# Retention and two feed-forward layers on one core: where the weight conversions and the retention stand, whose engine decays, and how wide the activations are

## The chip, the core and the metric

The kernel runs on one core of a Trainium2 chip. Its engines are TensorE (PE, matrix products; PEld is its weight load), VectorE (DVE), ScalarE (ACT), GpSimd (POOL) and SyncE (SP, which here issues all DMAs). They run side by side, each takes its own instructions strictly in a fixed order, and they wait for each other through semaphores. The metric is the device time of one execution in microseconds (us), as the median of several runs: 1741.69 us before (three runs, 1738.77 to 1744.80).

## What is computed

For 8 sequences of 576 tokens with 8 heads of 64 columns, the scores of q and k are scaled, multiplied by a decay that depends on the distance of two tokens, and multiplied with v (no softmax). The result, 4608 tokens of 512 columns, goes through two feed-forward layers of 2048 inner columns. The four weight matrices arrive as 64-bit floats (8.4 MB each).

```python
scores = scale * np.matmul(q, k.transpose(0, 1, 3, 2))
gamma = 1.0 - 2.0 ** (-5.0 - np.arange(H, dtype=np.float32))
Dmat = np.where(rel >= 0, gamma[:, None, None] ** rel[None, :, :], 0.0)
x = np.matmul(scores * Dmat, v)            # then (4608, 512)
h = x @ w1_in;  g = h - np.tanh(h);  x = g @ w1_out
h = x @ w2_in;  g = h * (1.0 / (1.0 + np.exp(-1.702 * h)));  out = g @ w2_out
```

## The kernel before, in words

**Retention.** Each sequence is cut into four chunks of 128 tokens and one of 64, so there are 40 chunks. A chunk is loaded (kT, qT, v, k: `att_load`), q and v are multiplied by powers of gamma on POOL (`att_decay`, lines 362 and 364), PE makes the scores pj (line 374), DVE multiplies them by the causal mask into pm (line 379), PE makes the output op from pm and v (391) and from the state S of the chunks in front (396), and the update up of S (413), which DVE adds (417). A chunk therefore waits for the one before it in its sequence through S. The output goes to DRAM (x_d), the first 512 tokens stay on the chip.

**Conversion of the weights.** DVE and ACT turn the two 32-bit words of each 64-bit weight into a 32-bit float, find each block's largest magnitude and split the block into two 16-bit parts, hi and lo. A unit is one DMA of 512 columns on 128 partitions (512 KB, 32 units a layer): ACT takes the magnitude (172), DVE clamps and shifts (177, 180), joins (187, 189), and later ACT writes hi (262) and DVE lo (263). After a block (four units) the largest value is spread over the partitions by POOL (`partition_all_reduce`, 121), and the small steps of `scale` (127 to 117) make a power of two from it. Layer 2 also forms sums of quarter blocks (221 to 224) for a scheme with seven products in place of eight, and its splits are lines 237 and 238.

**Layers.** Tokens are taken in 9 tiles of 512. In layer 1 a tile has 16 steps: 12 matmuls make h of 128 inner columns (541, three 16-bit products for each of four parts), ACT and DVE compute g = h - tanh(h) and split it (`act1`, lines 556 to 568), and 12 matmuls add it to the output (660), at least LAG = 2 steps later. In layer 2 a tile has 8 pair steps: 42 matmuls of 256 columns (587), `act2` (600 to 615), and 24 matmuls (637). Before a tile starts, its x is scanned, scaled and split (`prep_steps`).

**Order.** Before layer 1 stand the first FIRST = 4 chunks and the conversion of w1_in, 8 units in flight; its steps run under `urgent`. The conversion of w1_out and the other 36 chunks follow within layer 1: its first LAG0 = 8 steps carry the whole conversion of w1_out, also urgent, and mm_out starts after them; each step takes one or two of the three parts of a chunk. The conversion of layer 2 is spread over what is left of layer 1 but its last LAST2 = 20 steps, with one block buffer (`wb2`, bufs 1). A scheduler then fixes the order on each engine: by written order as priority, with an instruction moved up where its engine would else stand idle by the scheduler's own costs.

Of the kernel before, what the change touches and what calls it, by code (L numbers as in the profile page):

```python
# [49 lines left out]
FIRST = 4  # L50
LAST2 = 20
NIP = 3
NF1 = 3
NF0 = 8
LAG0 = 8
RATE0 = 2.0
RATE = 1.0
# [21 lines left out]
def retention_two_ffn(ctx: ExitStack, tc: tile.TileContext, q, k, v, w1i, w1o, w2i, w2o,  # L79
                      qt, kt, dq_d, dv_d, mask_d, out):  # L80
# [17 lines left out]
    tp = pool("tp", 2)  # L98
    ep = pool("ep", 4)
# [33 lines left out]
    for l in (1, 2):  # L133
        o = Obj()
        for nm, n in (("s_in", 4), ("inv_in", 4), ("s_out", 4), ("inv_out", 4), ("rs", 1), ("top", 16)):
            setattr(o, nm, cp.tile([P, n], F32, name=f"{nm}{l}"))
        o.wih, o.wil, o.woh, o.wol = {}, {}, {}, {}
        L[l] = o

    def conversion(l, kinds, w_in, w_out, fp, wb, wp):  # L140
# [5 lines left out]
        units = [(kind, b, u) for kind in kinds for b in range(4) for u in range(4)]  # L146
        f64s, blocks, red, sums = {}, {}, {}, {}

        def load(i):
            if i >= len(units):  # L150
                return
            kind, b, u = units[i]
            f = f64s[i] = fp.tile([P, 512, 2], I32, tag="f64", name="f64")
            if kind == "i":
                src = w_in.bitcast(I32)[:, b * 1024 + u * 256 : b * 1024 + u * 256 + 256]
            else:
                src = w_out.bitcast(I32)[u * 512 : u * 512 + 512, b * 256 : b * 256 + 256]
            SP.dma_start(f.rearrange("p (a b) c -> p a (b c)", a=4), src.rearrange("(a p) f -> p a f", p=P))

        def view(kind, w, u):  # L160
            return w[:, :, u * P : u * P + P] if kind == "i" else w[:, u * 4 : u * 4 + 4, :]

        def magnitude(i):
# [19 lines left out]
        def join(i):  # L183
            kind, b, u = units[i]
            wi = view(kind, blocks[kind, b][0], u).bitcast(I32)
            f = f64s.pop(i).rearrange("p (a b) c -> p a b c", a=4)
            V.scalar_tensor_tensor(out=wi, in0=f[:, :, :, 1], scalar=SIGN_TOP, in1=wi,  # L187
                                   op0=ALU.bitwise_and, op1=ALU.bitwise_or)
            V.scalar_tensor_tensor(out=wi, in0=f[:, :, :, 0], scalar=29, in1=wi,
                                   op0=ALU.logical_shift_right, op1=ALU.bitwise_or)  # L190

        def reduce(kind, b):
            mx = blocks[kind, b][1]
            if kind == "i":
                V.tensor_copy(out=o.top[:, 4 * b : 4 * b + 4], in_=mx)
# [51 lines left out]
        def split(kind, b, u):  # L247
            w = blocks[kind, b][0]
            if kind == "i":
# [14 lines left out]
            if u == 3:  # L264
# [13 lines left out]
    def conversion_steps(l, kinds, w_in, w_out, fp, nf, wb, ahead, wp, also=None):  # L278
# [4 lines left out]
        def start():  # L283
            for i in range(nf):
                load(i)
                if i == 1 and also:
                    also()
# [3 lines left out]
        for n, (kind, b) in enumerate(blocks):  # L291
            prev = blocks[n - 1] if n else None
            for u in range(4):
                i = 4 * n + u

                def one(i=i, u=u):
# [3 lines left out]
                    if ahead or u < 3:  # L300
# [16 lines left out]
            if not ahead or n == len(blocks) - 1:  # L317
# [5 lines left out]
                else:  # L323
                    steps += [lambda kind=kind, b=b, u=u: split(kind, b, u) for u in range(4)]
# [4 lines left out]
    x_done = [0]  # L329
    x_first = []  # L330
    early = [True]
# [5 lines left out]
    def att_load(b, n):  # L337
# [5 lines left out]
        for nm, src in (("kT", kt), ("qT", qt)):  # L343
            t = ip.tile([P, NPAIR, P], F32, tag=f"in_{nm}", name=f"{nm}_{b}_{n}", bufs=2 if nm == "kT" else NIP)
            SP.dma_start(t[:, :, :T], src[b, :, :, s0 : s0 + T].rearrange("h p s -> p h s"))
            setattr(a, nm, t)
        for nm, src in (("v", v), ("k", k)):
            if nm == "k" and n + 1 == len(CHUNKS):
                continue
            t = ip.tile([P, H, D], F32, tag=f"in_{nm}", name=f"{nm}_{b}_{n}")  # L350
            rows = src[b, :, s0 : s0 + T, :].rearrange("h p d -> p h d")
            if T == P:
                SP.dma_start(t, rows)
            else:
                for j in range(2):
                    SP.dma_start(t[64 * j : 64 * j + 64, :NPAIR, :], rows[:, j::2, :])
            setattr(a, nm, t)

    def att_decay(b, n):
        s0, T = CHUNKS[n]  # L360
        a = att[b, n]
        G.tensor_tensor(out=a.qT[:, :, :T], in0=a.qT[:, :, :T], in1=dq[:, :, s0 : s0 + T], op=ALU.mult)
        nh = H if T == P else NPAIR
        G.tensor_tensor(out=a.v[:, :nh], in0=a.v[:, :nh], in1=dv[:, n, :nh].to_broadcast([P, nh, D]), op=ALU.mult)

    def att_scores(b, n, pp):
# [9 lines left out]
        for s_ in pj:  # L376
            t = ap.tile([P, NPAIR, P], F32, tag="pm", name="pm", bufs=3)
# [4 lines left out]
    def att_values(b, n, pp):  # L382
# [39 lines left out]
        x_done[0] = g0 + T  # L422
# [122 lines left out]
    def act1(t, c, h):  # L545
# [3 lines left out]
        u = tp.tile([P, TT], F32, tag="u", name="u")  # L549
        w = tp.tile([P, TT], F32, tag="w", name="w")  # L550
        th = tp.tile([P, TT], F32, tag="t", name="t")
        d = tp.tile([P, TT], F32, tag="z", name="d")
        mk = tp.tile([P, TT], U8, tag="m", name="m")
        gh = gp[-1].tile([P, TT], F16, tag="gh", name="gh")
        gl = gp[-1].tile([P, TT], BF16, tag="gl", name="gl")
# [8 lines left out]
        gtile[1, t, c] = gh, gl  # L564
        A.activation(out=gh, in_=w, func=AF.Copy, scale=sg)  # L565

        def finish():
            V.scalar_tensor_tensor(out=gl, in0=w, scalar=sg, in1=gh, op0=ALU.mult, op1=ALU.subtract)  # L568

        return finish  # L570
# [21 lines left out]
    def act2(t, p, prods):  # L592
# [4 lines left out]
        h0 = tp.tile([P, TT], F32, tag="u", name="h0")  # L597
        h1 = tp.tile([P, TT], F32, tag="w", name="h1")
# [9 lines left out]
        for x, h in enumerate((h0, h1)):  # L608

            g = tp.tile([P, TT], F32, tag="tz"[x], name=f"g{x}")  # L610
            gh = gp[-1].tile([P, TT], F16, tag="gh", name="gh")
            gl = gp[-1].tile([P, TT], F16, tag="gl", name="gl")
# [8 lines left out]
    def mm_y(t, p):  # L621
# [9 lines left out]
        for m in range(4):  # L631
# [6 lines left out]
            if last:  # L638
                c = tp.tile([P, 4, P], F32, tag="z", name="c")
# [259 lines left out]
```

## Time and profile before

| | us |
|---|---|
| median of the runs (three) | 1741.69 |
| the profiled execution, its own time | 1743.8 |
| its span, first to last instruction | 1742.0 |
| PE busy in the span | 1632.8 (94%) |
| DVE busy | 1242.1 (71%) |
| ACT busy | 856.1 (49%) |
| POOL busy | 124.8 (7%) |

The profile is of one execution. The span leaves 1.8 us of its own time outside, and that execution is 2.1 us above the median. A row of a timeline gives an instruction's start and duration; two instructions of one engine overlap a little at their ends, so what one takes in a full row is the distance from its start to the next start. Busy time of a group counts each instant once.

### The profile page before, as it was taken

The page shows a single profiled execution, that of the slowest core. Times are in us where ns is not written, and L with a number is a line of the kernel's source. Part 1 is how long each engine was busy: PE and PEld are TensorE (multiplying, and loading weights), DVE is VectorE, ACT ScalarE, POOL GpSimd, SP SyncE. Part 2 cuts the span into 40 slices and gives each one's busy share as a digit, 9 for nine tenths or more (in the row PEclk, how much of TensorE's full clock was granted, in tenths as well). Part 3 has the DMA queues.
Part 4 walks back from the last instruction along what each step waited for, and adds up shares of the span by engine and source line. Part 5 has one row for each costly group of instructions (what it writes and reads, how often), then busy time and mean ns, then how long its engine had stood idle before and what let it go on. Part 6 is the DMA issues. An engine that isn't in the chain of part 4 may idle for free.

```text
span 1742.0 us, 26391 instructions
## 1 busy us (share of the span) xinstructions
PE 1632.8 (94%) x10429; PEld 929.1 (53%) x10512; DVE 1242.1 (71%) x2462; ACT 856.1 (49%) x1383; POOL 124.8 (7%) x120
## 2 busy tenths in 40 slices
PE   1468889999999999999999999999999999999998
PEld 1334444544544454454444456666666666666665
DVE  4779889869898978697797674747566574746453
ACT  1245466556665656566676663434434243434332
POOL 1222100111111111100000000000000000000000
PEclk7679999999999999999999999999999999999999
DMA  9347315344444535322510120101010010100000
GB/s 287 104 119 202 107 61 151 104 120 136 140 143 139 158 88 161 82 71 81 207 49 1 46 86 27 49 1 49 1 49 29 21 50 1 49 1 25 1 25 25
DMA packets 203132, 141.42 MB, mean 81 GB/s; under 512 B 109184, under 2 KB 187136, under 8 KB 200448
## 3 DMA queue, kind: packets, MB, share of 16 engines
q1 hardware_dynamic: 203008, 139.74, 26.7%
q8 instruction: 82, 1.34, 0.3%
q14 instruction: 42, 0.34, 0.1%
HBM read 100.91 MB, written 38.80 MB: 80 GB/s over the span
## 4 chain that ended last, share of the span: by engine, by line
PE 74%; DVE 14%; issue 4%; DMA 4%; ACT 1%; SPq 1%; POOL 1%; POOLq 0%; DVEq 0%
PE yp L637 21%; PE pr L587 19%; PE y L660 15%; PE h L541 14%; DVE w L563 1%; DVE gl L568 1%; DVE w L561 1%; DVE w L562 1%; PE op L391 1%; DVE d L560 1%; PE pj L374 1%; DVE w L187 1%; PE op L396 1%; DVE pm L379 1%; DVE w L177 1%
## 5 line engine op out<-in xcount | busy, mean ns | idle before, releaser
L587 PEld LDWEIGHTS <-ws 128*128 128x128 f16 x3024 | 295.9, 98 | 52.3
L541 PE MATMUL h<-xh,wih 128*128 128x512 f16 x576 | 220.2, 383 | 14.2 <-DVE d L560 8.5
L660 PE MATMUL y<-gh,wol 128*128 128x512 f16 x576 | 218.7, 380 | 4.7 <-issue 0.7
L541 PE MATMUL h<-xh,wil 128*128 128x512 f16 x576 | 220.1, 382 | 0.0
L541 PE MATMUL h<-xl,wih 128*128 128x512 f16 x576 | 220.0, 382 | 0.0
L637 PE MATMUL yp<-woh,gh 128*128 128x512 f16 x576 | 218.3, 379 | 0.0
L637 PE MATMUL yp<-wol,gh 128*128 128x512 f16 x576 | 218.3, 379 | 0.0
L637 PE MATMUL yp<-woh,gl 128*128 128x512 f16 x576 | 217.7, 379 | 0.0
L587 PE MATMUL pr<-th,ws 128*128 128x256 f16 x1152 | 212.5, 273 | 0.0
L660 PE MATMUL y<-gh,woh 128*128 128x512 f16 x576 | 200.8, 383 | 9.3 <-ACT gh L565 5.1
L613 ACT ACTIVATE g<-h,isig 128x512 f32<-128x512 f32 x144 | 102.1, 714 | 206.3 <-DVE h L605 206.2
L565 ACT ACTIVATE gh<-w,sg 128x512 f16<-128x512 f32 x144 | 103.9, 721 | 193.4 <-DVE w L563 176.9
L541 PEld LDWEIGHTS <-wih 128*128 128x128 f16 x1152 | 112.4, 98 | 149.9 <-issue 20.0
L660 PE MATMUL y<-gl,woh 128*128 128x512 bf16 x493 | 187.7, 381 | 1.6 <-DVE gl L568 1.4
L660 PEld LDWEIGHTS <-woh 128*128 128x128 f16 x1152 | 109.1, 98 | 138.1 <-issue 9.0
L637 PEld LDWEIGHTS <-gh 128*128 128x128 f16 x1152 | 112.7, 98 | 119.5
L587 PE MATMUL pr<-bh,ws 128*128 128x256 f16 x864 | 165.5, 273 | 0.0
L615 DVE SCALAR_TENSOR_TENSOR gl<-g,sg,gh 128x512 f16<-128x512 f32 x144 | 107.5, 750 | 75.8 <-ACT gh L614 75.7
L587 PE MATMUL pr<-tl,ws 128*128 128x256 f16 x576 | 157.0, 273 | 0.0
L560 DVE SCALAR_TENSOR_TENSOR d<-h,isig,t 128x512 f32<-128x512 f32 x144 | 107.3, 745 | 64.2 <-ACT t L557 64.1
L568 DVE SCALAR_TENSOR_TENSOR gl<-w,sg,gh 128x512 bf16<-128x512 f32 x144 | 115.6, 803 | 47.4 <-ACT gh L565 47.1
L601 DVE TENSOR_TENSOR h<-h,pr 128x256 f32<-128x256 f32 x72 | 30.2, 419 | 154.5 <-ACT h L600 154.5
(110 smaller groups left out, 2467.4 us busy)
## 6 DMA issues: line engine op xcount, KB each, us to landing
f<-in_moe_w_in SPq DMA_DIRECT2D x32, 512.0 KB, 5.1
f<-in_moe_w_out SPq DMA_DIRECT2D x32, 512.0 KB, 4.6
yd<-ev SPq DMA_DIRECT2D x36, 256.0 KB, 2.8
yf<-yd SPq DMA_DIRECT2D x9, 1024.0 KB, 4.8
out<-c SPq DMA_DIRECT2D x36, 256.0 KB, 2.0
kT<-t_k SPq DMA_DIRECT2D x32, 256.0 KB, 3.0
qT<-t_q SPq DMA_DIRECT2D x32, 256.0 KB, 3.5
v<-in_v SPq DMA_DIRECT2D x32, 256.0 KB, 4.0
```

Source lines behind the costliest of these rows:

```text
L177: V.tensor_scalar(out=w, in0=w, scalar1=HI_MOST, scalar2=HI_LEAST, op0=ALU.min, op1=ALU.max, accum_out=mx[:, u : u + 1])
L187: V.scalar_tensor_tensor(out=wi, in0=f[:, :, :, 1], scalar=SIGN_TOP, in1=wi, op0=ALU.bitwise_and, op1=ALU.bitwise_or)
L541: PE.matmul(h, w, x[:, kd, :], start=n == 0, stop=n == 3 * KD - 1)
L560: V.scalar_tensor_tensor(out=d, in0=h, scalar=isig, in1=th, op0=ALU.mult, op1=ALU.subtract)
L565: A.activation(out=gh, in_=w, func=AF.Copy, scale=sg)
L568: V.scalar_tensor_tensor(out=gl, in0=w, scalar=sg, in1=gh, op0=ALU.mult, op1=ALU.subtract)
L587: PE.matmul(ps, w, x[:, xi, k, :], start=i == 0, stop=i == 5)
L601: V.tensor_tensor(out=h0[:, l_], in0=h1[:, l_], in1=p2, op=ALU.add)
L613: A.activation(out=g, in_=h, func=AF.Gelu_apprx_sigmoid, scale=isig)
L615: V.scalar_tensor_tensor(out=gl, in0=g, scalar=j.sg[:, 0:1], in1=gh, op0=ALU.mult, op1=ALU.subtract)
L637: PE.matmul(y, a[:, cs], b, start=p == 0 and x == 0 and r == 0, stop=last and x == 1 and r == 2)
L660: PE.matmul(ys[m], a, b, start=first and i == 0, stop=last and i == 2)
```

## The change

Twenty chunks in place of four now stand before layer 1, with the conversions of both matrices of layer 1 (`"io"`), and the first tile's preparation; nothing is urgent any more. The other twenty chunks stand in the first twenty pair steps of layer 1, all three parts of a chunk in one step, and only behind them, when their buffers are free, does the conversion of layer 2 begin, now with two block buffers. A conversion unit is twice as wide (1 MB, 1024 columns; 16 units a layer; four in flight), with runs of 2 KB in DRAM for w_in. The host lays q, k and v out so that a chunk's tile has runs of 2 KB (1 KB in the short chunk) for each partition. The decay of q goes from POOL to DVE, that of v from POOL to eight pieces of 64 columns on ACT. Layer 1's activation works on pairs: the three instructions that read h stay at 512 columns, the other six take 1024; so do the last three of layer 2. The output's tiles c share two wide buffers.

```diff
-FIRST = 4
-LAST2 = 20
-NIP = 3
-NF1 = 3
-NF0 = 8
-LAG0 = 8
-RATE0 = 2.0
-RATE = 1.0
+FIRST = 20
+LAST2 = 10
+NIP = 4
+NF0 = 4
...
-        units = [(kind, b, u) for kind in kinds for b in range(4) for u in range(4)]
+        units = [(kind, b, u) for kind in kinds for b in range(4) for u in range(2)]
...
-            f = f64s[i] = fp.tile([P, 512, 2], I32, tag="f64", name="f64")
+            f = f64s[i] = fp.tile([P, 1024, 2], I32, tag="f64", name="f64")
...
+        if not b:
+            SP.dma_start(dq[:, :, s0 : s0 + T], dq_d[:, :, s0 : s0 + T])
+        for nm, src, h in (("kT", kt, NPAIR), ("qT", qt, NPAIR), ("v", v, H if T == P else NPAIR), ("k", k, H)):
...
-        G.tensor_tensor(out=a.qT[:, :, :T], in0=a.qT[:, :, :T], in1=dq[:, :, s0 : s0 + T], op=ALU.mult)
-        nh = H if T == P else NPAIR
-        G.tensor_tensor(out=a.v[:, :nh], in0=a.v[:, :nh], in1=dv[:, n, :nh].to_broadcast([P, nh, D]), op=ALU.mult)
+        V.tensor_tensor(out=a.qT[:, :, :T], in0=a.qT[:, :, :T], in1=dq[:, :, s0 : s0 + T], op=ALU.mult)
+        for h in range(H if T == P else NPAIR):
+            A.activation(out=a.v[:, h], in_=a.v[:, h], func=AF.Copy, scale=dv[:, n, h])
...
-    def act1(t, c, h):
+    def wide(tag, dt=F32, to=None, **kw):
...
+    def act1(t, c, hs):
+
         j = jobs[1, t]
         blk = c // 4
         isig, sg = j.isig[:, blk : blk + 1], j.sg[:, 0:1]
-        u = tp.tile([P, TT], F32, tag="u", name="u")
...
-        A.activation(out=u, in_=h, func=AF.Square, scale=isig)
-        A.activation(out=th, in_=h, func=AF.Tanh, scale=isig)
+        u, w, th, d, mk = wide("u"), wide("w"), wide("t"), wide("z"), wide("m", U8)
+        gh, gl = wide("gh", F16, gp[-1]), wide("gl", BF16, gp[-1])
+        for x, h in enumerate(hs):
+            A.activation(out=u[:, x], in_=h, func=AF.Square, scale=isig)
+            A.activation(out=th[:, x], in_=h, func=AF.Tanh, scale=isig)
+            V.scalar_tensor_tensor(out=d[:, x], in0=h, scalar=isig, in1=th[:, x], op0=ALU.mult, op1=ALU.subtract)
         A.activation(out=w, in_=u, func=AF.Square, scale=SQ, bias=sqb)
         A.activation(out=mk, in_=th, func=AF.Square, scale=MASK_SCALE)
-        V.scalar_tensor_tensor(out=d, in0=h, scalar=isig, in1=th, op0=ALU.mult, op1=ALU.subtract)
         V.scalar_tensor_tensor(out=w, in0=w, scalar=LEVEL, in1=u, op0=ALU.add, op1=ALU.mult)
         V.tensor_tensor(out=w, in0=w, in1=th, op=ALU.mult)
         V.copy_predicated(w, mk, d)
-        gtile[1, t, c] = gh, gl
         A.activation(out=gh, in_=w, func=AF.Copy, scale=sg)
...
+        V.scalar_tensor_tensor(out=gl, in0=w, scalar=sg, in1=gh, op0=ALU.mult, op1=ALU.subtract)
+        for x in range(2):
+            gtile[1, t, c + x] = gh[:, x], gl[:, x]
...
-
-            g = tp.tile([P, TT], F32, tag="tz"[x], name=f"g{x}")
-            A.activation(out=g, in_=h, func=AF.Gelu_apprx_sigmoid, scale=isig)
-            A.activation(out=gh, in_=g, func=AF.Copy, scale=j.sg[:, 0:1])
-            V.scalar_tensor_tensor(out=gl, in0=g, scalar=j.sg[:, 0:1], in1=gh, op0=ALU.mult, op1=ALU.subtract)
-            gtile[2, t, 2 * p + x] = gh, gl
+
+        A.activation(out=g, in_=h, func=AF.Gelu_apprx_sigmoid, scale=isig)
+        A.activation(out=gh, in_=g, func=AF.Copy, scale=j.sg[:, 0:1])
+        V.scalar_tensor_tensor(out=gl, in0=g, scalar=j.sg[:, 0:1], in1=gh, op0=ALU.mult, op1=ALU.subtract)
+        for x in range(2):
+            gtile[2, t, 2 * p + x] = gh[:, x], gl[:, x]
...
-        with ExitStack() as ps0:
-            fp = pool("fp", NF0, to=ps0, side="right")
-            wb = pool("wb", 2, to=ps0, side="right")
-            conv = conversion_steps(1, "i", w1i, w1o, fp, NF0, wb, True, wp1, constants)
-            pp = pool("ps0", 2, PSUM, to=ps0), {"s": "s", "v": "v", "u": "u"}
+        with ExitStack() as scope:
+            def constants():
...
+            fp = pool("fp", NF0, to=scope, side="right")
+            wb = pool("wb", 2, to=scope, side="right")
+            conv = conversion_steps(1, "io", w1i, w1o, fp, NF0, wb, True, wp1, constants)
+            pp = pool("ps0", 2, PSUM, to=scope), {"s": "s", "v": "v", "u": "u"}
             conv.popleft()()
...
+            jobs[1, 0].scale_y = scale_y
+            conv.extend(pre)
+            rate = len(conv) / (FIRST + 2)
...
-            for i in range(-2, len(chunks)):
-                acc += per
+            for i in range(-2, FIRST):
+                acc += rate
                 todo = int(acc)
...
-                if i + 2 < len(chunks):
+                if i + 2 < FIRST:
                     att_decay(*chunks[i + 2])
-                for _ in range(cuts[0]):
-                    urgent(conv.popleft())
-                if 0 <= i + 1 < len(chunks):
+                if 0 <= i + 1 < FIRST:
                     att_scores(*chunks[i + 1], pp)
-                for _ in range(cuts[1]):
-                    urgent(conv.popleft())
+                for _ in range(todo):
+                    conv.popleft()()
                 if i >= 0:
                     att_values(*chunks[i], pp)
...
+                att_load(*beyond[i + NIP])
...
+        tp = pool("tp", 2)
+        ep = pool("ep", 4)
+        gp.append(pool("gp", LAG + 1))
...
-        steps = [(1, t, c) for t in range(NTILE) for c in range(KF)]
-                l, t, c = steps[i]
-                fin = act1(t, c, mm_in(l, t, c, ps_h))
+        steps = [(t, p) for t in range(NTILE) for p in range(KF // 2)]
+                t, p = steps[i]
+                act1(t, 2 * p, [mm_in(1, t, 2 * p + x, ps_h) for x in range(2)])
+                if p == 1:
...
-                todo_a += RATE0 if early[0] else RATE
-                while bg and todo_a >= 1:
-                    wb = pool("wb2", 1, to=att_scope, side="right")
+                if bg:
+                    for _ in range(3):
+                        bg.popleft()()
+                elif conv2 is None:
+                    psa_scope.close()
+                    att_scope.close()
+                    fp = pool("fp2", 2, to=conv_scope, side="right")
+                    wb = pool("wb2", 2, to=conv_scope, side="right")
...
                     conv2 = conversion_steps(2, "io", w2i, w2o, fp, 2, wb, False, stg)
                     rate2 = len(conv2) / (n1 - LAST2 - i)
                 if conv2:
```

On POOL, at the start of the program, decays and all-reduces alternated (in `v_1_186` the first number is the chunk, and ISA without operands is a call that precedes the library's routine or the decay):

```order
L121 ISA
L121 ISA arw<-m_223 128x1
L362 ISA
L362 TENSOR_TENSOR qT_1_184<-qT_1_184,dq 128x512
L121 ISA
L121 ISA arw<-m_324 128x1
L364 ISA
L364 TENSOR_TENSOR v_1_186<-v_1_186,dv 128x512
```

In the changed kernel the same place reads:

```order
L115 ISA
L115 ISA arw<-m_235 128x1
L115 ISA arw<-m_354 128x1
L115 ISA arw<-m_562 128x1
L115 ISA arw<-m_700 128x1
L272 ISA rs_113<-m 128x1
```

The decays have left POOL; what is left there is one kind of instruction.

On PE, the first matmuls of layer 1 (line 541 before, 528 after) stood behind the first sequence and the first chunk of the second (`v_0_454`):

```order
L391 MATMUL op<-pm,v_4_373 64x64 x4
L396 MATMUL op<-qT_4_371,S 64x64 x2
L374 MATMUL pj_885<-qT_0_452,kT_0_450 128x128 x4
L374 MATMUL pj_886<-qT_0_452,kT_0_450 128x128 x4
L391 MATMUL op<-pm,v_0_454 64x128 x8
L413 MATMUL up<-v_0_454,k_0_456 64x64 x8
L541 LDWEIGHTS wih_0_266
L541 MATMUL h<-xh_0_615,wih_0_266 128x512
```

Now they stand behind the whole fourth sequence and the scores of the first chunk of the fifth (`qT_0_1432`):

```order
L379 MATMUL op<-pm,v_4_1364 64x64 x4
L384 MATMUL op<-qT_4_1362,S 64x64 x4
L379 MATMUL op<-pm,v_4_1364 64x64 x4
L384 MATMUL op<-qT_4_1362,S 64x64 x2
L362 MATMUL pj_1697<-qT_0_1432,kT_0_1430 128x128
L362 MATMUL pj_1698<-qT_0_1432,kT_0_1430 128x128
...
L528 LDWEIGHTS wih_0_286
L528 MATMUL h<-xh_0_1572,wih_0_286 128x512
```

Twenty chunks are in front of the first matmul of line 528, where six were in front of that of line 541.

On DVE, in the conversion of layer 2 inside layer 1, instructions of one conversion block stood between those of the activation (d, w, gl; `w_4843` is the block):

```order
L195 COPY top_126<-mx_4844 128x4
L197 TENSOR_REDUCE m_5376<-mx_4844 128x1
L189 SCALAR_TENSOR_TENSOR w_4843<-f_4903,w_4843 128x4x128
L568 SCALAR_TENSOR_TENSOR gl<-w,sg,gh 128x512
L562 TENSOR_TENSOR w<-w,t 128x512
L187 SCALAR_TENSOR_TENSOR w_4843<-f_5055,w_4843 128x4x128
L270 TENSOR_REDUCE tm<-top_126 128x1
L560 SCALAR_TENSOR_TENSOR d<-h,isig,t 128x512
L379 TENSOR_TENSOR pm<-pj_4543,mask_131 128x4x64
L563 COPY_PREDICATED w<-m,d 128x512
L561 SCALAR_TENSOR_TENSOR w<-w,u 128x512
```

In the changed kernel a like stretch (z is the former d, `w_5258` the block):

```order
L550 COPY_PREDICATED w<-m,z 128x1024
L108 TENSOR_SCALAR p_4991<-p_4991 128x1
L108 TENSOR_SCALAR p_5250<-p_5250 128x1
L236 SCALAR_TENSOR_TENSOR wsl<-wsum,s_in_115,wsh 128x1024
L175 TENSOR_SCALAR w_5258,mx_5259<-w_5258 128x4x256
L549 TENSOR_TENSOR w<-w,t 128x1024
L175 TENSOR_SCALAR w_5258,mx_5259<-w_5258 128x4x256
L109 TENSOR_SCALAR s_in_115<-p_4991 128x1
L111 TENSOR_SCALAR inv_in_116<-p_4991 128x1
L109 TENSOR_SCALAR sg<-p_5250 128x1
L111 TENSOR_SCALAR sg<-p_5250 128x1
L552 SCALAR_TENSOR_TENSOR gl<-w,sg,gh 128x1024
```

Before, the 32 units of layer 2 (line 177) are spread over the steps 17 to 94 of the 144 on DVE; now the 16 wide ones (line 175) stand between the pair steps 20 and 39 of the 72.

## Rows read from the trace of the kernel before

**Rows 1.** Busy time by stage, all engines; columns: window, length, engines, granted clock, DMA share, GB/s
```profile
0.00:100.00 100.00, 30.59 (x310) 24.10 (x312) 58.38 (x146) 22.99 (x38) 19.10 (x22) 0.68 0.69 189
160.00:300.00 140.00, 126.98 (x738) 62.64 (x749) 124.39 (x250) 81.58 (x133) 18.58 (x17) 0.98 0.42 120
300.00:860.00 560.00, 550.68 (x3516) 272.14 (x3571) 468.76 (x865) 340.96 (x556) 70.45 (x60) 1.00 0.43 127
860.00:1000.00 140.00, 139.37 (x647) 64.38 (x658) 111.37 (x184) 95.21 (x155) 1.90 (x2) 1.00 0.11 37
```
**Rows 2.** The chain that ended last, two pieces of layer 2: start, us, what
```profile
1072.17 5.18 PE yp L637 x24
1077.35 4.59 PE pr L587 x42
```
**Rows 3.** By stage, weight loads of line 541, then line 660, engine PEld
```profile
300.00:860.00 560.00, 101.81 (x1044) 1.00 0.43 127
...
300.00:860.00 560.00, 97.78 (x1045) 1.00 0.43 127
```
**Rows 4.** By stage, matmuls of line 391, engine PE
```profile
0.00:100.00 100.00, 10.44 (x86) 0.68 0.69 189
...
300.00:860.00 560.00, 33.15 (x416) 1.00 0.43 127
```
**Rows 5.** Waits of PE from 0 to 160 us: total, times, longest
```profile
PE pj L374 <- POOL qT L362: 50.2, 4, 16.5
```
**Rows 6.** Timeline of POOL: start, us, engine, line, operation [idle before, releaser]
```profile
26.77 0.38 POOL L121 PARTITION_ALL_REDUCE arw<-m  x1 [9.32 <-issue]
34.02 2.12 POOL L362 TENSOR_TENSOR qT<-qT,dq 128x512 f32<-128x512 f32 x1 [6.88 <-issue]
...
1119.85 0.35 POOL L121 PARTITION_ALL_REDUCE arx<-m  x1 [77.65 <-DVE m L458]
```
**Rows 7.** Timeline of DVE at 1119.5 us
```profile
1119.54 0.15 DVE L458 TENSOR_REDUCE m<-mxx 128x1 f32<-128x2 f32 x1
```
**Rows 8.** Timeline of DVE, a stretch without a gap
```profile
404.42 0.68 DVE L177 TENSOR_SCALAR_CACHE_REDUCE w<-w 128x512 f32<-128x512 f32 x1
...
405.02 0.68 DVE L561 SCALAR_TENSOR_TENSOR w<-w,u 128x512 f32<-128x512 f32 x1
405.63 0.75 DVE L180 TENSOR_SCALAR w<-w 128x512 int32<-128x512 int32 x2
406.30 0.74 DVE L568 SCALAR_TENSOR_TENSOR gl<-w,sg,gh 128x512 bf16<-128x512 f32 x1
...
407.56 1.28 DVE L187 SCALAR_TENSOR_TENSOR w<-f,w 128x512 int32<-128x512 int32 x2
408.77 0.74 DVE L560 SCALAR_TENSOR_TENSOR d<-h,isig,t 128x512 f32<-128x512 f32 x1
409.43 0.92 DVE L563 COPY_PREDICATED w<-m,d 128x512 f32<-128x512 uint8 x1
```
**Rows 9.** Timeline of DVE, then of POOL, at 390 us
```profile
390.35 0.87 DVE L238 SCALAR_TENSOR_TENSOR wsl<-w,s_in,wsh 128x256 f16<-128x256 f32 x2
391.14 1.28 DVE L238 SCALAR_TENSOR_TENSOR wsl<-wsum,s_in,wsh 128x1024 f16<-128x1024 f32 x1
392.34 3.08 DVE L238 SCALAR_TENSOR_TENSOR wsl<-w,s_in,wsh 128x256 f16<-128x256 f32 x3
...
391.30 2.25 POOL L362 TENSOR_TENSOR qT<-qT,dq 128x512 f32<-128x512 f32 x1 [10.55 <-DMA qT<-t_q]
```
**Rows 10.** Busy time of all engines in 5 us (columns as in rows 1)
```profile
10.00:15.00 5.00, 0.00 (x0) 0.00 (x0) 0.41 (x1) 0.00 (x0) 0.00 (x0) 1.00 1.02 350
```
**Rows 11.** Groups by line, one of ACT: count, busy us, mean ns, idle before
```profile
L419 ACT COPY S<-up 128x256 f32<-128x256 f32 x8 | 3.0, 369 | 0.0
```
**Rows 12.** By stage, matmuls of line 541, engine PE
```profile
100.00:120.00 20.00, 7.66 (x24) 0.70 0.31 80
```
**Rows 13.** Timeline, the last DVE instruction before the end
```profile
1737.77 1.34 DVE L640 TENSOR_TENSOR c<-yp,iy 128x512 f32<-128x512 f32 x2 [1.60 <-DMA out<-c]
```

More of the change, by code (lines that the diff above doesn't have):

```diff
@@ L283, in start @@
         def start():
+            if also:
+                also()
             for i in range(nf):
                 load(i)
-                if i == 1 and also:
-                    also()
             magnitude(0)
@@ L292, in conversion_steps @@
             prev = blocks[n - 1] if n else None
-            for u in range(4):
-                i = 4 * n + u
+            for u in range(2):
+                i = 2 * n + u
                 def one(i=i, u=u):
@@ L323, in conversion_steps @@
                 else:
-                    steps += [lambda kind=kind, b=b, u=u: split(kind, b, u) for u in range(4)]
+                    steps += [lambda kind=kind, b=b, u=u: split(kind, b, u) for u in range(2)]
         return deque(steps)
     att = {}
-    x_done = [0]
     x_first = []
-    early = [True]
     def ps_tile(pp, stage, name):
@@ L638, in mm_y @@
             if last:
-                c = tp.tile([P, 4, P], F32, tag="z", name="c")
+                if m % 2 == 0:
+                    both = wide("z")
+                c = both[:, m % 2].rearrange("p (b d) -> p b d", b=4)
                 V.tensor_tensor(out=c, in0=y.rearrange("p (b d) -> p b d", b=4), in1=iy, op=ALU.mult)
-                SP.dma_start(out[t * TT + m * P : t * TT + m * P + P, :], c.rearrange("p b d -> p (b d)"))
+                SP.dma_start(out[t * TT + m * P : t * TT + m * P + P, :], both[:, m % 2])
         if last:
@@ L690, in tile_slots @@
     def tile_slots(t):
-        sp = xp if t % 2 else wp2[0]
-        return [(sp, tag + (str(x) if t % 2 == 0 else "")) for x in range(2) for tag in ("xh", "xl")]
+        if t % 2:
+            return (xp, "xh"), (xp, "xl"), (xp, "xh"), (xp, "xl")
+        return (wp1, "wih0"), (wp1, "wil0"), (wp1, "wih1"), (wp1, "wil1")
     chunks = [(b, n) for b in range(B) for n in range(len(CHUNKS))]
-    later = chunks[FIRST:]
-    chunks = chunks[:FIRST]
-    beyond = chunks + later + [(B, 0)] * 8
+    beyond = chunks + [(B, 0)] * NIP
     if True:
-        def urgent(f):
-            with tc.high_priority(offset=URGE):
-                f()
+        gp = []
         att_scope = ctx.enter_context(ExitStack())
@@ L768, in retention_two_ffn, with first @@
         bg = deque()
-        for i, ch in enumerate(later):
-            nxt = beyond[len(chunks) + i + 3]
-            def first(ch=ch, nxt=nxt):
-                att_load(*nxt)
+        for i, ch in enumerate(chunks[FIRST:]):
+            def first(ch=ch, nxt=beyond[FIRST + i + NIP - 1] if i else None):
+                if nxt:
+                    att_load(*nxt)
                 att_decay(*ch)
@@ L887 @@
         add(f"in_{name}", a.view(np.int64) if a.dtype == np.float64 else a)
[L888 to L891 removed]
+    for name, turned in (("q", True), ("k", True), ("k", False), ("v", False)):
+        x = np.asarray(inputs[name])
+        rows = []
+        for s0, T in CHUNKS:
+            c = x[:, :, s0 : s0 + T]
+            if turned:
+                c = c.reshape(B, NPAIR, 2, T, D).transpose(0, 2, 4, 1, 3)
+            elif T == P:
+                c = c.transpose(0, 2, 1, 3)
+            else:
+                c = c.reshape(B, NPAIR, 2, T, D).transpose(0, 2, 3, 1, 4)
+            rows.append(c.reshape(B, T * DM))
+        add(f"{'t' if turned else 'n'}_{name}", np.ascontiguousarray(np.concatenate(rows, axis=1)))
     for name, a in const_arrays().items():
```

204 lines of the change are left out of this document (69 added, 135 removed).

## The prediction

> **What bounds the kernel now.** I read four views in this order. First the busy time by stage: from 300 us on PE is busy in 550.7 of 560 us, then in 139.4 of 140, while up to 100 us it is busy in only 30.6 of 100 [rows 1]. So PE's work sets the end, and a change can only move the time in which PE does none of it. Second, what that work takes: 24 matmuls of 512 columns 5.18 us, a pair's 42 of 256 columns 4.59 [rows 2]. Layer 1 is 144 steps of 5.18 us (12 + 12 matmuls), 746 us; layer 2 is 72 pairs of 4.59 + 5.18, 703 us. In 300 to 860 us stand 1044 + 1045 weight loads of the two layer lines [rows 3], 451 us of matmuls, and 416 of the 16 records that line 391 has a chunk [rows 4], 26 chunks: (550.7 - 451) / 26 = 3.84 us a chunk on PE. The floor is 746 + 703 + 40 x 3.84 = 1603 us. The span of 1742 lies 139 above it.
>
> Third, where these 139 us are. Up to 100 us line 391 has 86 records, 5.4 chunks, 21 us of the floor's work: 79 lost. From 300 to 860: 9.3. At the end about 6 (the last evictions wait and store from 1737.8 on [rows 13]). The difference, 45, fell between 100 and 300, where the conversion of w1_out ran beside layer 1's activation and DVE was busy in 124.4 of the last 140 us [rows 1]. Fourth, why: PE waited 50.2 us for POOL's decay of q in four waits [rows 5], and POOL itself did nothing then: each change between its decays and its all-reduce has 6 to 9 us in front of it in which nothing is waited for that the profile shows [rows 6]. With no decay near, the all-reduce starts 0.2 us behind the DVE instruction that feeds it [rows 6, 7]. [...]
>
> **The change, part by part.** Since the PE floor stays at 1603 us, I add up what PE loses.
>
> *Before layer 1* (P us long, with 20 chunks x 3.84 = 77 us of the floor's work in it). DVE carries most. Distances in a full row of it give 0.60 us for 512 columns (177, 561 and each 187), 0.34 for 180, 0.66 for d and gl [rows 8], 1.20 for 1024 columns of a lo, 0.40 for 256 [rows 9]. So 1024 columns of a 0.60 take 1.13 (0.53 more for 512 elements), of a 0.34 0.61. A unit of 1024 is 1.13 + 0.61 + 1.13 + 1.13 + 1.20 = 5.2 us, 16 units 83. By the new order, up to the decay that the first FFN matmul stands behind, DVE also has 33 masks and 21 decays (46 whole at 0.60, 8 short at 0.33: 30), 10 state sums (3.4), six scans and four lo of x (11.5), and some 86 one-column steps (0.1 each, 9): 137 us in all. The first unit is queued behind the first chunk on SP, so some 8 us pass first. With no further gap P is 145. As in the first 100 us, where DVE is 58.4% busy [rows 1], it would be 236. I take the 89% of 160 to 300 us [rows 1], since the POOL gaps are gone and the rest of the ping-pong is of that kind: 145 / 0.89 = about 164. Loss 164 - 77 = 87.
> The eight pieces of v on ACT have no row; the copy of 256 columns at 0.37 us [rows 11] is the nearest, and bounds a piece at 0 and 0.37. At the upper end ACT has 18 x 8 x 0.37 = 53 us of them, 47 of conversion (32 x 4 x 0.37), 15 of copies: 115, under P, so DVE hides it; value taken, nothing. DMA moves up to there 16.8 MB of weights, 18.4 of chunks, 7 of others; at the 350 GB/s of [rows 10] 120 us, at the 189 of the first 100 us 223. I take it as hidden, since 2 KB runs replace those of 256 and 512 bytes and rows 10 fell into loads of w_in in runs of 1 KB.
>
> *Layer 1's start.* The first 24 matmuls of h took 7.66 us before [rows 12], 2.5 more than at full clock; with as much again for the first pair's wait for its own buffers: 5 (0 to 10).
>
> *The first 20 pair steps* carry a chunk each: PE 20 x (10.36 + 3.84) = 284 us, DVE 161. Lost at the rate of 300 to 860 us, 9.3 in 560 [rows 1]: 5. No decay in this stage is on POOL; before, a POOL decay beside DVE stretched three lo from 0.40 to 1.03 us [rows 9], so I count DVE with the undisturbed durations.
>
> *The conversion of layer 2.* The order puts all 16 wide units between the pair steps 20 and 40, though the written order would spread them to step 62. I counted DVE there: 40 d at 0.66, 59 wide w and gl at 1.13 to 1.19 and 20 copies at 1.15 (117 with d), 45 wide 177/187/189 and 16 wide 180 (61), 24 lo of 256 and 12 of 1024 (24), 16 sums at 0.34, four scans and four lo of x, 80 small ones (28): 230 us. PE has 20 x 10.36 = 207. PE can run ahead of DVE by no more than its two h buffers, so at least 23 - 5 = 18 us are lost; at 89% busy DVE would take 258, a loss of 51. I take 28: DVE nearly full, as its list is long and never waits for POOL. Before, the same work was spread over twice the time, at 468.8 of 560 [rows 1], and cost 9.3.
>
> *The last 30 pair steps* have DVE at 6 of 10.36: 1 (0.6 in 140 us [rows 1]). *Layer 2* had no wait of PE before and its wide instructions start no later than h1 did: 0. *The end*: four c in two wide buffers don't wait for a store: 6 - 1.6 [rows 13] = 4.4.
>
> Sum: 87 + 5 + 5 + 28 + 1 + 4 = 130 us over the floor, span 1733, against 1742: 9 us less. With the 1.8 outside the span the profiled execution's 1743.8 would be 1734.8; on the median's scale (1741.69, 2.1 lower) 1733.
>
> **Rivals.** *The chain of the retention sets P.* [...] It decides from 8.2 us a chunk on (164 / 20). [...] Against: scores of the next chunk need no state and overlap. Chance 0.25, slower.
> *DVE in the conversion of layer 2 falls further behind*, since each 1 MB load must land, and ACT take its magnitude, while units are used up at one in 13 us through two buffers: 51 in place of 28, 1756 us. Chance 0.1, slower.
> *The conversion only fills gaps there*, and the clustered order costs as little as before, 4: 1709 us. Against it is the sum of 230 for 207. Chance 0.15.
> *The 2 KB runs don't raise the rate*, and the stage before layer 1 is bound by DMA at 189 GB/s: 223, 1792 us. Against: 350 in rows 10. Chance 0.05.
> My forecast has the remaining 0.45, with its own range 1716 to 1750 (P from 150 to 178, the conversion from 22 to 34).
>
> **How the numbers follow.** What a measurement can tell from no change is about 0.3%, 5 us: under 1736.5 is faster, over 1746.9 slower. Of my forecast's 0.45 I count 0.29 faster, 0.09 the same, 0.07 slower; the gap-filling rival is faster (0.15); of the chain's 0.25, which can be milder, 0.05 faster, 0.06 the same, 0.14 slower; of the other two's 0.15 nearly all slower. In all 0.50 faster, 0.16 the same, 0.34 slower. The range takes in the gap-filling rival and both slower ones up to the chain's own bound, and leaves out the DMA rival: 1704 to 1776.
>
> **What would show it.** Right: the first matmul of line 528 at 155 to 175 us with DVE near 89% busy before it; no POOL gap of 6 us behind a max; PE gaps ended by DVE's z or by ACT between pair steps 20 and 40 (some 28 us, from about 460 us on), with DVE over 95% busy; no PE wait behind; the end without a wait for out<-c. [...]

## The result, and the profile of the changed kernel

The changed kernel takes 1726.63 us (median of 4 runs, 1723.94 to 1728.2), the kernel before, beside it, 1741.09: a ratio of 0.9913, 95% interval 0.9891 to 0.9935, some 14.5 us less. The forecast was 1733. The profiled execution has a span of 1726.4 us. The first view is the busy time by stage, with the columns of [rows 1]:

```profile
0.00:100.00 100.00, 68.80 (x634) 54.82 (x634) 87.29 (x162) 55.05 (x126) 4.70 (x11) 0.71 0.88 296
100.00:140.00 40.00, 27.90 (x254) 21.95 (x255) 36.33 (x75) 23.46 (x60) 4.13 (x3) 0.70 0.72 213
140.00:180.00 40.00, 31.75 (x334) 22.98 (x334) 20.84 (x55) 17.47 (x56) 0.70 (x2) 0.83 0.69 218
300.00:460.00 160.00, 160.00 (x1172) 81.63 (x1171) 102.39 (x117) 93.70 (x163) 0.00 (x0) 1.00 0.29 86
460.00:700.00 240.00, 222.16 (x1005) 98.88 (x1004) 239.99 (x390) 168.23 (x215) 14.74 (x12) 0.99 0.38 123
700.00:1000.00 300.00, 300.00 (x1392) 136.02 (x1391) 220.34 (x266) 183.59 (x233) 1.38 (x4) 1.00 0.19 64
```

In the first 100 us PE is busy in 68.8 us (30.6 before [rows 1]) and DVE in 87.3 (58.4). From 300 us to 1000 PE has no gap except from 460 to 700, where DVE is busy in 239.99 of 240 us: the conversion of layer 2. The second view is the line of layer 1's first matmul (count, shortest, median and longest in ns, first and last start), up to 300 us:

```profile
L528 PE MATMUL h<-xh,wih x80: 376/379/390, 170.6 to 297.9; 128*128 128x512 f16 x80
```

The third is PE's waits (total, times, longest), up to 180 us and then from 180 to 960; no wait for POOL is left, where [rows 5] had 50.2 us:

```profile
PE up L401 <- ACT v L352: 16.4, 3, 10.7
PE pj L362 <- DVE pm L367: 15.7, 7, 4.1
PE pj L362 <- DVE qT L350: 8.5, 2, 7.4
PE op L384 <- DVE S L405: 5.0, 2, 4.7
...
PE y L643 <- DVE gl L552: 8.9, 4, 3.5
PE h L528 <- DVE z L545: 5.6, 6, 2.0
PE y L643 <- ACT gh L551: 4.6, 5, 3.1
```

Behind four settings of constants at the start, POOL's timeline has only all-reduces up to 180 us, where [rows 6] had 6 to 9 us of idle for "issue" at each change between them and the decays. In front of this one DVE's m ended the wait:

```profile
48.44 0.35 POOL L115 PARTITION_ALL_REDUCE arw<-m  x1 [19.28 <-DVE m L195]
```

Over the floor of 1603 us the span has lost 123 us (139 before). The 170.6 us before layer 1 hold 20 chunks (320 matmuls of line 379) and the scores of the next, 78 us of the floor: 93 lost. From 170.6 to 300 PE idles 4.0 us. From 460 to 700 stand 1004 matmuls of the two layer lines at 0.216 us, 217 of 240 us: 23 lost, of which 18 are gaps and some 5 went to matmuls that took longer than 0.216. The end costs about 4: PE stops, and DVE's last outputs, which wait for nothing but PE, are still to be made and stored. These make 124.

```profile
1722.59 0.69 DVE L623 TENSOR_TENSOR z<-yp,iy 128x512 f32<-128x512 f32 x1 [0.17 <-PE yp L618]
```

### The profile page after: what moved, and what is told of

It reads as the page before. It is cut to its first block, busy times and chain, and to the rows that moved or that the text cites. A ratio compares the mean times of both kernels' runs of the same rounds, so it can differ in the third digit from the quotient of the medians.

```text
span 1726.4 us, 25486 instructions
## 1 busy us (share of the span) xinstructions
PE 1651.0 (96%) x10512; PEld 951.0 (55%) x10512; DVE 1184.4 (69%) x1966; ACT 848.1 (49%) x1263; POOL 28.5 (2%) x40
## 4 chain that ended last, share of the span: by engine, by line
PE 78%; DVE 16%; DMA 3%; issue 2%; ACT 1%; SPq 0%; DVEq 0%; ACTq 0%
PE yp L618 21%; PE pr L570 19%; PE y L643 17%; PE h L528 16%; PE pj L362 2%; PE op L379 2%; DVE w L187 1%; DVE w L185 1%; PE op L384 1%; DVE w L175 1%; DVE z L545 1%; DVE w L550 1%; DVE wsl L236 1%; DVE w L548 1%; DVE w L549 1%
## 5 line engine op out<-in xcount | busy, mean ns | idle before, releaser
L643 PE MATMUL y<-gl,woh 128*128 128x512 bf16 x576 | 219.1, 380 | 8.9 <-DVE gl L552 8.9
L593 ACT ACTIVATE w<-u,isig 128x1024 f32<-128x1024 f32 x72 | 82.6, 1148 | 271.4 <-DVE u L591 271.4
L643 PE MATMUL y<-gh,woh 128*128 128x512 f16 x576 | 209.5, 380 | 4.6 <-ACT gh L551 4.6
L595 DVE SCALAR_TENSOR_TENSOR gl<-w,sg,gh 128x1024 f16<-128x1024 f32 x72 | 92.4, 1283 | 131.7 <-ACT gh L594 131.6
L545 DVE SCALAR_TENSOR_TENSOR z<-h,isig,t 128x512 f32<-128x512 f32 x144 | 107.8, 750 | 87.4 <-ACT t L544 87.2
L543 ACT ACTIVATE u<-h,isig 128x512 f32<-128x512 f32 x144 | 98.2, 682 | 119.5 <-PE h L528 119.3
L551 ACT ACTIVATE gh<-w,sg 128x1024 f16<-128x1024 f32 x72 | 82.6, 1148 | 135.2 <-DVE w L550 116.4
L552 DVE SCALAR_TENSOR_TENSOR gl<-w,sg,gh 128x1024 bf16<-128x1024 f32 x72 | 92.5, 1284 | 48.0 <-ACT gh L551 46.8
```

The source lines that it names most:

```text
L543: A.activation(out=u[:, x], in_=h, func=AF.Square, scale=isig)
L545: V.scalar_tensor_tensor(out=d[:, x], in0=h, scalar=isig, in1=th[:, x], op0=ALU.mult, op1=ALU.subtract)
L643: PE.matmul(ys[m], a, b, start=first and i == 0, stop=last and i == 2)
```

## The experiments

All ratios are to the kernel before, which ran beside each.

**Decays back on POOL** (one part undone).

```diff
-        V.tensor_tensor(out=a.qT..., in1=dq[:, :, s0 : s0 + T], op=ALU.mult)
-        for h in range(H if T == P else NPAIR):
-            A.activation(out=a.v[:, h], in_=a.v[:, h], func=AF.Copy, scale=dv[:, n, h])
+        G.tensor_tensor(out=a.qT..., in1=dq[:, :, s0 : s0 + T], op=ALU.mult)
+        nh = H if T == P else NPAIR
+        G.tensor_tensor(out=a.v[:, :nh], ..., in1=dv[:, n, :nh].to_broadcast([P, nh, D]), op=ALU.mult)
```

> The changed kernel with the decays of q and v back on POOL (the two tensor_tensor of the kernel before), nothing else. Up to layer 1 POOL then has 42 decays at about 2.1 us (89 us) and ten all-reduces among them, each with a change of code in front and one behind. Theory (each change costs POOL 6 to 9 us, and taking the decays off POOL is where the gain before layer 1 came from): POOL needs some 89 + 20 x 7 = 229 us before the first matmul of line 528, which comes at 220 to 240 us in place of 171; the time is 1775 to 1800 us. [...]

Measured: 1804.98 us, ratio 1.037 (1.0351 to 1.0389). The first FFN matmul, PE's waits up to 240 us, and POOL's timeline around one all-reduce:

```profile
L528 PE MATMUL h<-xh,wih x40: 376/380/391, 245.3 to 297.4; 128*128 128x512 f16 x40
```
```profile
PE up L401 <- POOL v L352: 38.4, 4, 16.9
PE pj L362 <- DVE pm L367: 35.4, 5, 7.8
PE pj L362 <- POOL qT L350: 25.4, 3, 15.6
```
```profile
130.45 2.25 POOL L350 TENSOR_TENSOR qT<-qT,dq 128x512 f32<-128x512 f32 x1
138.67 0.38 POOL L115 PARTITION_ALL_REDUCE arw<-m  x1 [5.97 <-issue]
145.83 1.03 POOL L352 TENSOR_TENSOR v<-v,dv 128x512 f32<-128x512 f32 x1 [6.78 <-issue]
146.84 1.27 POOL L350 TENSOR_TENSOR qT<-qT,dq 128x512 f32<-128x512 f32 x1
...
179.05 0.38 POOL L115 PARTITION_ALL_REDUCE arw<-m  x1 [6.19 <-issue]
179.78 0.35 POOL L115 PARTITION_ALL_REDUCE arx<-m  x1 [0.35 <-DVE m L445]
```

One all-reduce of 0.38 us costs POOL 13 us: 6 in front and 7 behind. Up to 240 us there are 12 of them in 11 stretches. In front of eight stretches the gap is 5.8 to 6.2 us (the other three waited for something else too), and behind all eleven it is 6.7 to 8.8. Where an all-reduce follows an all-reduce, as at 179.78, or a decay a decay, as at 146.84, there is no such gap: it goes with the change. The decays, 0.6 to 2.3 us each, are 54 us of POOL's time there (42 of them), where the theory had 89; so its 229 us came close with one term too large. Start and time lie a little past the theory's ranges. With the long runs and the split of the work kept, the time is 78 us above the changed kernel's 1727, so it was not these that made the gain before layer 1. What the expectation calls a change of code is, in these rows, a step from a decay to an all-reduce or back; what POOL does in the gap no row shows.

**The decays moved in the kernel before** (that one part alone; the edit above the other way round).

> The kernel before with one part of the change alone: the decay of q on DVE and that of v in eight pieces on ACT, nothing on POOL but the all-reduces; order, split, runs and widths as before. Theory (the loss before layer 1 came from POOL's changes of code): the 50 us that PE waited for POOL's q go for the most part, and 40 decays at 0.60 us (24 us) on a DVE that was busy in 124 of 140 us beside the conversion of w1_out give some of it back: 1700 to 1725 us. Rival (what helped was the order, with half of the retention in front, and the long runs): within 5 us of before, 1736 to 1746.

Measured: 1694.78 us, ratio 0.9733 (0.9712 to 0.9753): beyond what the theory gave, 32 us faster than the whole change. The first FFN matmul, up to 100 us by stage, and PE's waits up to 300 us:

```profile
L541 PE MATMUL h<-xh,wih x128: 376/379/634, 77.6 to 296.3; 128*128 128x512 f16 x128
```
```profile
0.00:100.00 100.00, 60.63 (x494) 41.93 (x496) 87.11 (x220) 59.19 (x140) 5.61 (x11) 0.88 0.86 230
```
```profile
PE up L413 <- ACT v L364: 14.1, 1, 14.1
PE pj L374 <- DVE qT L362: 10.2, 2, 7.5
```

Layer 1 starts at 77.6 us in place of 107.8, the waits for POOL are gone, and nothing was given back beside the conversion of w1_out: from 160 to 300 us PE is busy in 137.5 of 140 us, where it was 127.0 [rows 1]. With the two runs the change splits into its decays and the rest:

| | decays on POOL | on DVE and ACT |
|---|---|---|
| order, runs and widths of before | 1741 | 1695 |
| those of the change | 1805 | 1727 |

The decays are worth 47 us in the order of before and 78 in the new one; the rest of the change costs 64 and 32. The runs below take those 32 apart.

**The conversion of layer 2 spread** over the pair steps as written, to see whether its cluster is the price.

```diff
             w = view(kind, blocks[kind, b][0], u)
+            if l == 2:
+                A.copy(out=w[:, 0, 0:1], in_=newest[-1][:, 0, 0:1])   # newest gh of layer 1
             A.activation(out=w, in_=words(i, f64s[i], 1).bitcast(F32), func=AF.Abs)
```

> The changed kernel, where the first ACT instruction of each conversion unit of layer 2 is preceded by a one-column ACT copy from the newest gh, so that a unit can't be moved ahead of the pair step it is written in: the 16 units lie between the pair steps 21 and 58 instead of 20 and 39. The same work, 113 us of DVE, over twice the steps. Theory (the loss of some 23 us between 450 and 700 us is DVE's sum, 230 us against PE's 207): it falls to 2 to 6, time 1704 to 1712 us, PE busy over 99% from 450 to 900 us. Rival (it comes from single waits behind long conversion instructions, each of which delays one activation): the waits are the same in number, only further apart, 1722 to 1728 us.

Measured: 1702.66 us, ratio 0.9781 (0.9763 to 0.9799), 24 us less than the changed kernel. By stage:

```profile
460.00:700.00 240.00, 240.00 (x1114) 108.81 (x1113) 227.08 (x344) 167.88 (x229) 15.21 (x9) 1.00 0.26 93
700.00:900.00 200.00, 200.00 (x928) 90.65 (x927) 173.97 (x241) 133.34 (x170) 12.80 (x6) 1.00 0.36 113
```

The same work costs nothing over the pair steps 21 to 58, where it stood in 20 to 39 (451 to 670 us): PE has no gap at all up to 900 us, and all 23 us come back (a little more than the theory's 1704 to 1712 us). The rival falls.

**Activation in pieces of 512** (the pairs undone, in act2 too).

```diff
-        V.tensor_tensor(out=w, in0=w, in1=th, op=ALU.mult)     # and the other wide instructions
+        for x in range(2):
+            V.tensor_tensor(out=w[:, x], in0=w[:, x], in1=th[:, x], op=ALU.mult)
```

> The changed kernel with every activation instruction of 1024 columns cut into two of 512 (both layers, ACT and DVE), same buffers. A DVE instruction of 512 costs 0.60 and one of 1024 1.13, so 4 x 0.07 = 0.28 us more DVE work per pair of layer 1. Theory (DVE sets the pace while layer 2's weights are converted, and nowhere else): 20 pairs x 0.28 = 5.6 us more, 1731 to 1734 us, the added loss between 450 and 700 us. Rival (the waits there are latency of the chain act to matmul, which shorter instructions make shorter): 1715 to 1726 us.

Measured: 1734.6 us, ratio 0.9962 (0.9947 to 0.9977), 8 us more than the changed kernel. In the clustered stage:

```profile
460.00:700.00 240.00, 219.84 (x974) 96.93 (x973) 239.08 (x452) 169.62 (x265) 18.67 (x10) 0.96 0.38 123
```

973 weight loads of the layers got through in place of 1004, so 31 matmuls less, 6.7 us at 0.216. Another 0.9 us of PE's time is idle from 300 to 460 us, where the changed kernel had no gap. The time is just past the theory's range; the rival, shorter waits, falls. The granted clock is 0.96 in the clustered stage.

**Short runs of q, k and v** (their layout in memory and their loads as before).

```diff
-            x = src[b, s0 * DM : (s0 + T) * DM].rearrange("(p h x) -> p h x", p=P, h=h)
-            SP.dma_start(t[:, :, :T] if nm[1:] else t[:, :h], x)
+            SP.dma_start(t[:, :, :T], src[b, :, :, s0 : s0 + T].rearrange("h p s -> p h s"))   # q, k turned
+            SP.dma_start(t, src[b, :, s0 : s0 + T, :].rearrange("h p d -> p h d"))             # v, k
```

> The changed kernel with q, k and v laid out in memory as in the kernel before (runs of 256 and 512 bytes in place of 2 KB), the weights' loads unchanged. Theory (POOL was the limit, transfers had room): the DMA rate of the first 100 us falls below 296 GB/s but the first matmul of line 528 stays within 10 us of 171; time 1725 to 1740 us. Rival (the gain came from the longer runs: with the short ones the stage before layer 1 goes at the 189 GB/s of before): 42 MB take 223 us, the first matmul at about 220, time 1770 to 1785 us.

Measured: 1734.32 us, ratio 0.9961 (0.9949 to 0.9973).

```profile
0.00:100.00 100.00, 59.95 (x544) 48.20 (x544) 83.81 (x153) 50.37 (x108) 7.44 (x11) 0.71 1.03 278
```
```profile
L536 PE MATMUL h<-xh,wih x73: 376/380/632, 176.6 to 299.6; 128*128 128x512 f16 x73
```

The rate falls from 296 to 278 GB/s, not to 189, at a DMA share of 1.03 in place of 0.88; layer 1 starts 6 us later. The long runs are worth 8 us in this order, and the low rate of before was not that of its short runs: in the kernel before with its decays moved, the same runs went at 230.

**Scans of x behind layer 1's start.** In the last 30 us before layer 1 DVE is idle for 12, and waits in order (DVE, then PE):

```profile
157.64 2.35 DVE L441 TENSOR_REDUCE mxx<-yf 128x1 f32<-128x1024 f32 x2 [3.77 <-DMA yf<-xd]
159.90 0.41 DVE L405 TENSOR_TENSOR S<-up,S 128x256 f32<-128x256 f32 x1
...
160.37 0.69 PE L384 MATMUL op<-qT,S 64*64 64x128 f32 x4 [4.68 <-DVE S L405]
```

DVE stands at a scan of tile 2 whose transfer isn't in, with the state sum S that PE waits for behind it.

```diff
         def reduce(i):
+            if l == 1 and t in (1, 2) and i == 0:
+                V.tensor_copy(out=j.mx[:, 0:1], in_=newest[-1][:, 0, 0:1])
```

> The changed kernel, where the scan of x's tiles 1 and 2 is preceded by a one-column DVE copy from the newest gh, so that DVE can't take it before layer 1 has begun: up to the first matmul of line 528 DVE has two scans less in front of the state sums, and the 3.4 and 3.8 us for which DVE waited there for x's transfer are gone. Theory (in the last 30 us before layer 1 the in-order DVE holds the retention's chain): the first matmul of line 528 comes at 160 to 165 us in place of 171, time 1716 to 1722. Rival (that tail is set by the chunks themselves, 6.8 us each at the lower clock, whatever DVE does between): it stays at 168 to 172, time 1724 to 1729.

Measured: 1722.65 us (1718.79 to 1727.51), ratio 0.9893 (0.9873 to 0.9913); the first FFN matmul at 159.4 us. The 11 us at the start are there as the theory said, but the interval overlaps that of the changed kernel, and the median lies between the two forecasts: what the time gains is not settled. The rival's 6.8 us a chunk are the changed kernel's own: PE is busy in 68.80 of its first 100 us, with 162 matmuls of op, 10.1 chunks, at a granted clock of 0.71. (The profiled execution is the fastest of the six.)

**15 and 10 chunks in front**, with the edits of the spread run and of the late scans.

```diff
-FIRST = 20
+FIRST = 15      # in the other run 10
```

> The changed kernel with the conversion of layer 2 spread over the pair steps as written (as in the run spread), the scans of tiles 1 and 2 behind layer 1's start (as in late_scan), and 15 chunks in place of 20 in front of layer 1. Theory (DVE's sum sets the time before layer 1): 118 us of work and 8 at the start, at 89% busy 141 us; loss 141 - 15 x 3.84 = 83 in place of 93, and the conversion's 23 gone: 1690 to 1696 us. Rival (the chunks' chain at the lower clock sets it, 6.8 us each): 15 chunks and 8 us are 110 us, and with the conversion's own 110 us of DVE in parallel the first FFN matmul comes at 120 to 125: 1672 to 1680 us.

> As best15 with 10 chunks in front of layer 1; the conversion of layer 2 has 32 pair steps. Theory (DVE's sum sets the time before layer 1, and a chunk moved behind layer 1's start takes some 2 us off DVE but 3.84 us of PE's work out of the stage): DVE 108 us and 8, 130 us at 89%; loss 130 - 38 = 92, and DVE in the 32 pairs has 5.85 x 32 + 113 = 300 of 331 us, loss 2 to 5: 1698 to 1706 us, slower than best15. Rival (the chunks' chain sets it): the stage shrinks by another 34 us, against 19 of work moved: 1660 to 1668, faster than best15.

Measured: 1687.8 us with 15, ratio 0.9693 (0.967 to 0.9715), the best of all versions; 1696.24 with 10, ratio 0.9734 (0.9711 to 0.9757). First FFN matmul, 15 then 10:

```profile
L533 PE MATMUL h<-xh,wih x101: 377/379/631, 130.5 to 299.5; 128*128 128x512 f16 x101
```
```profile
L533 PE MATMUL h<-xh,wih x107: 379/379/634, 131.5 to 299.5; 128*128 128x512 f16 x107
```

Five chunks fewer in the edit don't start layer 1 any earlier, with DVE busy in 118.6 and 115.4 of the first 131 us. But they are not five on PE. The matmuls of op, 16 a chunk (line 382), up to 131 us, 15 then 10:

```profile
0.00:131.00 131.00, 29.93 (x240) 0.73 0.87 288
0.00:131.00 131.00, 26.39 (x208) 0.66 0.83 270
```

So 15 chunks stand in front in the one run and 13 in the other: the scheduler moved three up. With the same start, the run with 10 has two chunks less of PE's work behind it, 2 x 3.84 = 7.7 us, and it is 8.4 us slower. Five more come behind the start of 15: with 20 (and the late scans) layer 1 started at 159.4, 29 us later, for 5 x 3.84 = 19 of PE's work. So, by these starts, some 15 chunks fit beside the conversion of layer 1. The run with 15 started between what its theory (141 us) and its rival (120 to 125) gave, and its time is 2 us under the theory's range and 8 over the rival's. The rival's 1660 to 1668 us with 10 isn't seen, but its condition was met only in part; what 10 chunks alone in front would give is not shown.

Of the 32 us that the rest of the change cost, spreading the conversion returns 24; with the late scans and 15 chunks the new order is 7 us better than that of before with its decays moved (the two intervals just touch).

**The order of before, with the decays moved and the long runs**, and with 8 chunks in front.

```diff
+        if not b:
+            SP.dma_start(dq[:, :, s0 : s0 + T], dq_d[:, :, s0 : s0 + T])
+            x = src[b, s0 * DM : (s0 + T) * DM].rearrange("(p h x) -> p h x", p=P, h=h)
+            SP.dma_start(t[:, :, :T] if nm[1:] else t[:, :h], x)
-FIRST = 4
+FIRST = 8       # in the second run alone
```

> The run before_decay with the changed kernel's layout of q, k, v in memory and its loads (runs of 2 KB, q's factors by chunks); order, split and widths as in the kernel before. Theory (the long runs are worth the 8 us that taking them away cost in the run short_runs): 1684 to 1690 us. Rival (there DVE, busy 87 of the first 100 us, is the limit, and the transfers at 230 GB/s have room): 1692 to 1697 us.

> As decay_long, with 8 chunks in place of 4 in front of layer 1. Theory (DVE's sum sets the time to the first FFN matmul; a chunk put in front of it takes some 2.1 us of DVE there, 2.4 at 89% busy, and carries 3.84 us of PE's work): 4 x 1.4 = 6 us less than decay_long. Rival (DVE is as full behind layer 1's start, so that what is done earlier is only exchanged; chunks at the lower clock cost PE 6 us): within 3 us of decay_long, or slower.

Measured: 1695.18 us, ratio 0.974 (0.9722 to 0.9759), and 1694.86, ratio 0.9734 (0.9717 to 0.9751): both rivals hold. The long runs are worth nothing where DVE, not the transfers, fills the first 100 us (DVE is busy in 88.4 of them with the long runs and in 87.1 with the short, at 230 GB/s with either). In the second run layer 1 starts at 92.0 us in place of 75.4. Up to there stand these matmuls of op (line 385), 4 then 8 chunks in the edit:

```profile
0.00:75.40 75.40, 12.95 (x96) 0.75 0.83 261
0.00:92.00 92.00, 18.91 (x130) 0.82 0.78 249
```

They are 6 and 8 chunks, since the scheduler had moved two up: 16.6 us later for some 8 of PE's work. The times are equal all the same, so the rest comes back behind the start.

## Why the prediction was right, step by step

Its time was 6 us high, in the same direction as the result, and its mechanism held: the POOL gaps were the loss before layer 1, and DVE set the pace after they were gone. That it came so near is in part luck: the loss before layer 1 was forecast 6 us too low, the other terms together 12 too high.

- *Before layer 1*: 164 us forecast, 170.6 measured; loss 93 for 87. The list of DVE's work was right: it ends with the decay that starts at 160.2 us, and up to its end at 160.9 DVE is busy in 137.2 us (137 forecast). What the forecast put at nothing is what PE does behind that decay, the rest of the last chunks: 9.7 us, without a gap and below the full clock. The 89% was not one rate either. DVE's first conversion instruction starts at 13.8 us, where 8 were forecast (the weights' first transfer is issued at 5.7, behind the first chunk's, into a stretch of 343 GB/s at a share of 0.97); then DVE is busy in 96% up to 140 us, and in 65% from there to its list's end, behind x's transfers. The sign "near 89% busy" was missed: it is 83% up to layer 1. The two stretches, all engines:

```profile
13.80:140.00 126.20, 90.77 (x841) 71.53 (x841) 121.56 (x232) 74.02 (x175) 8.64 (x10) 0.68 0.84 273
160.90:170.60 9.70, 9.70 (x145) 7.31 (x144) 4.70 (x22) 4.28 (x17) 0.35 (x1) 0.85 0.57 159
```

The chain rival's own bound, the upper end of the range (1776 us), was the author's estimate, and no run shows it; measured were 170.6 us for the stage, with DVE and not the chain setting the pace up to 140, and a tail in which PE and DVE did wait for each other, which the late scans shortened by 11 us.
- *The pieces of v on ACT*, costed at nothing between 0 and 0.37 us: a group of eight takes 2.02 us, 0.25 each. Of PE's waits before layer 1, 16.4 us end on them, the longest with 10.7, but that is no price of the pieces: ACT itself waited for v's transfer (ACT, then PE):

```profile
23.69 2.02 ACT L352 ACTIVATE v<-v,dv 128x64 f32<-128x64 f32 x8 [1.75 <-DMA v<-n_v]
24.53 1.71 PE L401 MATMUL up<-v,k 128*64 128x64 f32 x16 [10.72 <-ACT v L352]
```

Up to layer 1 ACT waited 28.4 us, in 13 times, for transfers of v.
- *The conversion of layer 2*: 28 forecast, 23 measured, and shown by the spread run to be the cluster alone. The bounds 18 and 51 held it; DVE was 100% busy, where 28 assumed nearly so. The rival that it only fills gaps is what the spread order does, not this one; that DVE falls further behind (51) was not seen. Only 18 of the 23 are gaps; the other 5, matmuls that took longer, stood in no term of the sum.
- *Layer 1's start, the first 20 pairs, the end*: 5, 5 and 4.4 forecast; 4, 0 and 4 measured. At the end no c waits for a store any more.
- *The rival that the long runs don't help*: the first 100 us ran at 296 GB/s, and with short runs at 278. The 189 of before was the rate that POOL's gaps left, and no property of the runs: the same runs went at 230 once the decays had left POOL.

What the prediction did not see is that its largest gain and its largest loss were separate decisions. It summed the new order, and never priced the decays alone in the old one: 1695, 32 us better than the order that it summed.

## What to carry to other kernels

Price each part of a change in the old order too: here one part gave 47 us, and the others took 32 of them back. Before handing POOL two kinds of instructions, count the changes between them: here 54 us of decays and 5 of all-reduces filled 240 us. Where a scheduler may move work ahead, work that fits on average can still be put where the engine is full; a one-column dependency on the newest result of the main loop holds it in place, and gave 24 us. For the same reason, count in the trace what really stands in front: an edit from 15 chunks to 10 moved two.

## What the runs showed of the hardware beyond that

TensorE's granted clock was 0.50 in a stretch where PE was busy in 10.14 of 11 us, as in the 20 us before it with PE busy in 9.87, in the run with 10 chunks (columns of [rows 1]):

```profile
100.00:120.00 20.00, 9.87 (x62) 7.30 (x64) 18.90 (x30) 11.29 (x29) 0.70 (x2) 0.50 0.58 173
120.00:131.00 11.00, 10.14 (x72) 7.76 (x69) 9.62 (x34) 6.80 (x14) 1.18 (x1) 0.50 0.41 125
```

From 460 to 700 us its mean fell inside layer 1 where PE had waits: 1.00 with PE busy in 240.00 us (spread), 0.99 in 222.16 (changed kernel), 0.96 in 219.84 (narrow), and 0.96 in 224.71 (short runs), so the busy time alone doesn't order them. A wait cost more than its own length there: the narrow run idles 20.2 us, and its 973 matmuls, 210 us at 0.216, leave 29.8 of 240. Against the changed kernel (17.8 and 23) it has 2.3 us more of gaps and loses 6.7; the difference goes with the lower clock, but no run separates it.
